# A planning constant for when the rows of a finished transfer may be used: 3.5 in place of 1.5 microseconds

## The chip, the cores and the metric

The kernel runs on one core of a Trainium2 chip. The metric is the device time of one execution in microseconds. Times are medians of several executions of the same program.

## The reference, cut to what matters

```python
def reference(x, w1d):                       # x: (1, 384, 384, 384) bf16, w1d: (1,)
    g = jnp.einsum("bhwc->bc", x) / (H * W)  # mean over all 147456 pixels, per channel
    s = _sigmoid(g * w1d[0])
    return x * s[:, None, None, :]           # every pixel scaled by its channel's gate
```

All of x (113 MB) has to be read before the first output can be written, and SBUF, the on-chip memory, holds only a part of it. So there are two passes: pass one reads everything and sums it, and keeps 367 of the 1152 rows per partition in SBUF (some of them packed four into three); pass two stores the kept rows, scaled, and loads, scales and stores the other 785 once more. A "row" below is 384 channels on 128 partitions, 98304 bytes.

## The kernel before

Loads and stores all go out on one queue, in the order in which the program adds them. The queue stops at the first transfer whose wait isn't met yet. A load into rows of the arena (the block of SBUF rows that all transfers share) waits until the store that last read them has landed; a store waits until VectorE has scaled its rows.

```python
def load(chunk, a, lo, hi):
    r0, n = chunk
    fl.add("SP",
        lambda: nc.sync.dma_start(out=arena[:, a : a + hi - lo, :], in_=view(xf, r0, n)[:, lo:hi, :]),
        writes=rows(a, hi - lo), dma=True)

def store(chunk, a, lo, hi):
    r0, n = chunk
    return fl.add("SP",
        lambda: nc.sync.dma_start(out=view(of, r0, n)[:, lo:hi, :], in_=arena[:, a : a + hi - lo, :]),
        reads=rows(a, hi - lo), dma=True)
```

`fl.add` works out the waits from the rows that a step reads and writes, so every order is safe. Which order it is, a plan decides while the program is built. It steps through pass two in its own time `now`, with a list `moves` of transfers that drain at a fixed rate:

```python
ROW, PER_LOAD, PER_STORE = 0.2267, 0.112, 0.061
LAT, SEEN, DT = 2.0, 1.5, 0.05
...
while True:
    ...                                   # VectorE: scale a landed chunk, or unpack a kept group
    while waiting and waiting[0][0] <= now:
        _, n, then, chunk, a, lo, known = waiting.popleft()
        known.append(store(chunk, a, lo, lo + n))
        moves.append([now + LAT, n * ROW + PER_STORE, then])
    ...
    while over and over[0][0] <= now:
        over.popleft()[1]()               # a store is over: its rows are idle, or a load has landed
    ...
    if got and todo < N_STREAM:
        n, a = max(got)                   # the longest run of idle rows
        n = min(n, CAP, N_STREAM - todo)
        ahead = backlog()
        if n >= BIG or n == N_STREAM - todo or (ahead < LOW and n >= 8) or ahead < LAST:
            load(STREAMED, a, todo, todo + n)
            ...
    if moves and moves[0][0] <= now:
        moves[0][1] -= DT
        if moves[0][1] <= 0:
            over.append((now + SEEN, moves.popleft()[2]))
    ...
    now += DT
```

`SEEN` is the time that the plan lets pass between the end of a transfer and the use of its rows. It holds for both kinds: for a store, until its rows may be loaded into, and for a load, until VectorE may be given its rows.

## Time and profile before

| | before |
|---|---|
| median, 6 executions | 722.3 us (721.88 to 723.66) |
| span of the profiled execution | 721.3 us |
| moved | 303.87 MB, 421 GB/s on average |
| first and last data packet of pass two | 271.8 and 718.9 us |

The prediction below shows the views and says how each is read. One thing in advance: a transfer is divided among 16 DMA engines. The trace has every packet (one partition's part of a transfer) with its start and its duration, and every increment of a transfer's semaphore; a transfer has landed when the last of the 16 increments stands. From these records I take three quantities: how long the packets of each size usually take, which packets took over 40 ns longer (called slow), and the time between the first and the last of the 16 increments of one transfer (called the spread).

### The profile page before, as it was taken

The numbers are of one execution on the slowest core, as the hardware profiler recorded it, in microseconds if no ns is written. First come the engines' busy times: TensorE is split into PE (matmuls) and PEld (weight loads), VectorE is DVE, ScalarE is ACT, GpSimd is POOL, SyncE is SP. The second block draws the span as 40 slices with busy tenths as digits, with TensorE's granted clock in tenths as the row PEclk, the third lists the DMA queues.
The fourth block names the chain that finished last, engine by engine and source line by source line (L and its number), as shares of the span: only waits on it lengthen the run. The fifth ranks groups of instructions, "written<-read, shape, count | busy, mean of one in ns | idle before, by whom it ended". The sixth has DMA issues, their size and how long they took to land.

```text
span 721.3 us, 3240 instructions
## 1 busy us (share of the span) xinstructions
PE 214.6 (30%) x1202; PEld 119.2 (17%) x1202; DVE 496.3 (69%) x470; ACT 115.4 (16%) x92; POOL 0.2 (0%) x4
## 2 busy tenths in 40 slices
PE   4677788897987770000000000000000000000000
PEld 2344445554543430000000000000000000000000
DVE  4600004788899819989799999999996992558500
ACT  3600003566677610002000000000000000000000
POOL 0000000000000000000000000000000000000000
PEclk9799999999899995555555555555555555555555
DMA  9999999999999978999999999999999999999997
GB/s 382 429 443 424 425 435 430 431 433 433 424 427 427 428 320 341 425 430 426 403 430 436 428 438 430 429 439 433 432 432 439 423 445 431 432 430 433 435 436 306
DMA packets 18882, 303.87 MB, mean 421 GB/s; under 512 B 2098, under 2 KB 2098, under 8 KB 4658
## 3 DMA queue, kind: packets, MB, share of 16 engines
q1 hardware_dynamic: 18864, 303.67, 98.6%
q8 instruction: 9, 0.15, 0.1%
q14 instruction: 7, 0.06, 0.0%
q10 hardware_dynamic: 2, 0.00, 0.0%
HBM read 190.41 MB, written 113.25 MB: 421 GB/s over the span
## 4 chain that ended last, share of the span: by engine, by line
DMA 55%; DVE 28%; PE 6%; ACT 5%; SPq 0%; issue 0%; another core or an unknown queue 0%; DVEq 0%
DMA arena<-in_x_dram 38%; DVE arena L441 19%; DMA out_dram<-arena 17%; DVE arena L265 6%; PE bank L241 6%; ACT arena L302 5%; DVE arena L271 3%; SPq L235 0%; ACT s_bf L432 0%; SPq L762 0%; DVEq L112 0%; SPq L106 0%
## 5 line engine op out<-in xcount | busy, mean ns | idle before, releaser
L441 DVE TENSOR_TENSOR arena<-arena,s_bf 128x1536 bf16<-128x1536 bf16 (+8 forms) x103 | 242.3, 2391 | 59.0 <-DMA arena<-in_x_dram 42.0
L265 DVE TENSOR_SCALAR arena<-arena 128x1536 uint16<-128x1536 uint16 (+2 forms) x247 | 145.5, 634 | 113.4 <-DMA arena<-in_x_dram 100.8
L241 PE MATMUL bank<-arena,ones 128*128 128x384 bf16 x1152 | 206.5, 341 | 52.7 <-DMA arena<-in_x_dram 52.6
L241 PEld LDWEIGHTS bank<-arena,ones 128*128 128x128 bf16 x1152 | 114.3, 102 | 144.6 <-DMA arena<-in_x_dram 58.7
L271 DVE TENSOR_TENSOR arena<-arena 128x1536 uint16<-128x1536 uint16 (+2 forms) x114 | 121.2, 1063 | 6.7 <-PE bank L241 4.4
L302 ACT ACTIVATE arena<-arena 128x3072 uint16<-128x3072 uint16 (+1 forms) x38 | 102.5, 2698 | 142.3 <-DVE arena L265 142.3
L514 PE MATMUL bank<-odd,ones 128*128 128x1 bf16 x1 | 0.2, 184 | 329.4 <-DVE odd L509 329.4
L514 PEld LDWEIGHTS bank<-odd,ones 128*128 128x128 bf16 x1 | 0.1, 103 | 329.8 <-DVE odd L509 329.8
L375 ACT COPY arena<-bank 128x512 uint32<-128x512 uint32 (+1 forms) x7 | 4.0, 571 | 61.8 <-DMA out_dram<-arena 61.6
L256 PE MATMUL bank<-ones,zeros 128*128 128x384 bf16 x48 | 8.3, 326 | 0.0
L302 ACT ACTIVATION_READ_ACCUMULATOR arena<-arena 128x1 f32 x38 | 7.1, 188 | 0.0
L256 PEld LDWEIGHTS bank<-ones,zeros 128*128 128x128 bf16 x48 | 4.7, 98 | 3.1
L375 ACT COPY bank<-arena 128x512 uint32<-128x512 uint32 (+1 forms) x7 | 3.6, 565 | 0.0
L432 ACT ACTIVATE s_bf<-bank,w_sc 128x384 bf16<-128x384 f32 x1 | 0.6, 581 | 15.4 <-PE bank L241 15.4
L735 ACT ACT_TABLE_LOAD x1 | 1.3, 1283 | 0.7 <-PEq L751 0.7
L332 DVE TENSOR_SCALAR w_sc<-bank 128x1 f32<-128x1 f32 x1 | 0.2, 159 | 1.1 <-PE bank L327 1.1
L322 DVE MEMSET ones<- 128x128 bf16 x1 | 0.2, 165 | 1.0 <-SPq L106 1.0
L327 PE MATMUL bank<-w_bf,ones 1*128 1x1 bf16 x1 | 0.2, 182 | 2.1 <-DMA w_bf<-in_w1d_dram 2.1
L327 PEld LDWEIGHTS bank<-w_bf,ones 1*128 1x128 bf16 x1 | 0.1, 100 | 2.1 <-DMA w_bf<-in_w1d_dram 2.1
L518 DVE CAST odd_i<-bank 128x1 int32<-128x1 f32 x1 | 0.2, 159 | 0.3 <-PE bank L514 0.3
L504 DVE TENSOR_REDUCE worst<-seen 128x1 f32<-128x38 f32 x1 | 0.2, 185 | 0.0
L509 DVE TENSOR_SCALAR odd<-worst 128x1 bf16<-128x1 f32 x1 | 0.2, 156 | 0.0
(5 smaller groups left out, 0.5 us busy)
## 6 DMA issues: line engine op xcount, KB each, us to landing
arena<-in_x_dram SPq DMA_DIRECT2D x15, 4608.0 KB, 33.9
arena<-in_x_dram SPq DMA_DIRECT2D x22, 1248.0 KB, 11.6
out_dram<-arena SPq DMA_DIRECT2D x8, 3072.0 KB, 30.3
arena<-in_x_dram SPq DMA_DIRECT2D x6, 3072.0 KB, 27.3
out_dram<-arena SPq DMA_DIRECT2D x12, 1248.0 KB, 11.8
out_dram<-arena SPq DMA_DIRECT2D x3, 4608.0 KB, 39.8
arena<-in_x_dram SPq DMA_DIRECT2D x3, 4512.0 KB, 37.9
out_dram<-arena SPq DMA_DIRECT2D x3, 4512.0 KB, 27.7
```

What stands on the lines that cost most here:

```text
L241: return nc.tensor.matmul(acc, lhsT=ones[:], rhs=arena[:, i, :], start=first, stop=last)
L256: lambda: nc.tensor.matmul(acc, lhsT=zeros[:], rhs=ones[:, None, :].to_broadcast([P, C // P, P]), start=False, stop=False),
L265: lambda: nc.vector.tensor_scalar(out=dst, in0=src, scalar1=s0, scalar2=s1, op0=op0, op1=op1),
L271: "DVE", lambda: nc.vector.tensor_tensor(out=dst, in0=a, in1=b, op=op), reads=reads, writes=writes
L302: lambda: nc.scalar.activation(out=y, in_=y, func=ACTF.Copy, accum_out=seen[:, 2 * k + i : 2 * k + i + 1]),
L322: fl.add("DVE", lambda: nc.vector.memset(ones[:], 1.0), writes=["ones"])
L327: lambda: nc.tensor.matmul(votes, lhsT=ones[0:1, :], rhs=w_bf[0:1, 0:1], start=True, stop=True),
L375: "ACT", lambda: nc.scalar.copy(dst.bitcast(u32), src.bitcast(u32)), reads=reads, writes=writes
L432: lambda: nc.scalar.activation(out=s_bf[:], in_=acc, func=ACTF.Sigmoid, scale=w_sc[:, 0:1]),
L441: lambda: nc.vector.tensor_tensor(out=v, in0=v, in1=s_bf[:, None, :].to_broadcast([P, n, C]), op=Op.mult),
L514: lambda: nc.tensor.matmul(votes, lhsT=ones[:], rhs=odd[:], start=True, stop=True),
L735: nc.scalar.preload_act_table(ACTF.Sigmoid)
```

## The change

The plan is to let 3.5 us pass before a store's rows count as free, so that loads come later in the queue, behind more stores, and hold it up less. The same constant also puts off the moment at which the plan counts a load as landed, and with it the order of VectorE's work.

```diff
-    LAT, SEEN, DT = 2.0, 1.5, 0.05
+    LAT, SEEN, DT = 2.0, 3.5, 0.05
```

## The prediction

> **What bounds the kernel now.** I read the page first (sections 2 and 4), then the busy time by stretch, then the waits of the DMA queue, then single microseconds where the transfer rate dips. The page's slices of one fortieth of the span:
>
> ```profile
> DVE  4600004788899819989799999999996992558500
> DMA  9999999999999978999999999999999999999997
> GB/s 382 429 443 424 425 435 430 431 433 433 424 427 427 428 320 341 425 430 426 403 430 436 428 438 430 429 439 433 432 432 439 423 445 431 432 430 433 435 436 306
> ```
>
> The DMA engines are full everywhere but in the first slice, at the turn from pass one to pass two (slices 15 and 16) and in the last one. VectorE is nearly full in the first two thirds of pass two, so it has to be kept in view. The same by stretch (busy time of each engine, then granted clock, DMA share, GB/s):
>
> ```profile
> 18.00:264.00 246.00, 200.62 (x1130) 111.83 (x1131) 130.13 (x180) 103.86 (x79) 0.00 (x0) 0.94 1.00 430
> 264.00:272.00 8.00, 5.25 (x32) 2.75 (x29) 2.02 (x3) 0.58 (x1) 0.00 (x0) 1.00 0.30 120
> 272.00:290.00 18.00, 0.00 (x0) 0.00 (x0) 17.96 (x13) 0.00 (x0) 0.00 (x0) 0.50 0.96 373
> 290.00:600.00 310.00, 0.18 (x1) 0.10 (x1) 292.79 (x249) 4.00 (x7) 0.00 (x0) 0.50 1.01 430
> 600.00:708.00 108.00, 0.00 (x0) 0.00 (x0) 45.12 (x14) 0.00 (x0) 0.00 (x0) 0.50 1.00 434
> 708.00:721.30 13.30, 0.00 (x0) 0.00 (x0) 0.00 (x0) 0.00 (x0) 0.00 (x0) 0.50 0.61 261
> ```
>
> Pass two (from 272 us) runs at 430 to 434 GB/s except in its first 18 us (373) and its last 13. TensorE's halved clock means nothing here: it has no work. VectorE is busy 293 of 310 us up to 600, but only 45 of 108 after that; it is done 40 us before the end.
>
> The waits of the queue that issues all transfers, in pass two (who waited for whom: us in total, times, longest):
>
> ```profile
> SPq L451 <- DVE arena L441: 240.5, 44, 29.0
> SPq L235 <- DMA out_dram<-arena: 145.2, 28, 17.3
> ```
>
> The second line is what the change aims at: 28 loads stand 145 us in the one in-order queue until the store of their rows has landed. That looks like a third of pass two, but the engines stay full meanwhile, since transfers issued earlier are still queued: these waits are hidden. Single microseconds at the dips (same columns):
>
> ```profile
> 277.00:278.00 1.00, 0.00 (x0) 0.00 (x0) 1.00 (x1) 0.00 (x0) 0.00 (x0) 0.50 1.12 313
> 278.00:279.00 1.00, 0.00 (x0) 0.00 (x0) 1.00 (x1) 0.00 (x0) 0.00 (x0) 0.50 0.78 215
> 279.00:280.00 1.00, 0.00 (x0) 0.00 (x0) 1.00 (x2) 0.00 (x0) 0.00 (x0) 0.50 0.82 240
> 280.00:281.00 1.00, 0.00 (x0) 0.00 (x0) 1.00 (x1) 0.00 (x0) 0.00 (x0) 0.50 0.86 227
> ...
> 347.00:348.00 1.00, 0.00 (x0) 0.00 (x0) 1.00 (x3) 0.00 (x0) 0.00 (x0) 0.50 0.96 255
> 716.00:717.00 1.00, 0.00 (x0) 0.00 (x0) 0.00 (x0) 0.00 (x0) 0.00 (x0) 0.50 0.34 147
> ```
>
> There the share is high and the rate low: the packets themselves are slow. At 277 to 281 us they are the 6144-byte packets of the first load of pass two (234 ns is usual, many took 446, some over 1000), at 344.5 to 350 the 9984-byte packets of another small load (375 usual, up to 1428). In the last microseconds the 16 engines end one after the other.
>
> **What the Trainium skill says.** "DMA: Bandwidth & Descriptors", section "Where 436 GB/s comes from", gives a ceiling of 435 GB/s for the 16 ports and says that for HBM to SBUF a limit of some 358 binds. The trace agrees with the first and not with the second: a 36864-byte packet takes 1364 ns on one of 16 engines, 432 GB/s, and whole stretches run at 434. Section "Anatomy of one DMA" puts a fixed cost of about 2 us on a transfer, most of it the receipt from the target memory. The trace shows less at the end of a store: the last data packet of the kernel ends at 718.87 us and the last increment of its semaphore stands at 719.20, 0.33 us later; the queue's next load starts 0.02 us after such an increment. Section "Queues, rings and completion order" says that each engine consumes its ring in order and that the increments of one transfer come from up to 16 engines separately. The trace agrees, and this matters: the 16 increments of one store come within 0.16 us at the start of pass two, but 2.5 us apart after the slow load at 277 us and 3.9 us apart after the one at 345 us, and they stay so to the end (715.34 to 719.20). The plan's constant must therefore cover 0.35 us of receipt plus this spread, which makes 3.5 us a more honest figure than 1.5.
>
> **The change part by part.** The constant is used only in the plan that is made while the program is built; nothing waits for it on the chip. It can act in one way, through the order and the sizes of transfers and VectorE instructions. Comparing the two built programs: TensorE, ScalarE and GpSimd have the same order, so have pass one and the start of pass two; the first difference is that the first load moves behind one more 8-row store. Everything up to about 275 us is out of reach.
> Bytes: in both plans 1152 rows (of 98304 bytes) are stored and 785 loaded in pass two, 190.4 MB. Nothing is saved there.
> Number of transfers in pass two: 82 before, 86 after (loads 30 to 32, stores 52 to 54). Packets of 6144 and 36864 bytes take 234 and 1364 ns, so a byte costs 0.0368 ns on one engine and a packet 8 ns besides; a transfer is 8 packets and a 9 ns increment per engine, some 0.075 us beyond its bytes. Four more make +0.3 us, on the path, since the engines are the bound.
> VectorE: the same instructions but for the cuts, in another order; no sum changes by more than about a microsecond of the 358 busy in pass two, and it has 93 us of slack.
> Distance of the loads: counting the rows that stand in the queue between a load and the nearest store that it waits for, before has 16 and 23 as its smallest, then 34, with a median of 49.5; after has 24, 26, 30, 34 and a median of 61. At 434 GB/s a row takes 0.2267 us, so the smallest cover goes from 3.6 to 5.4 us. Against the 0.35 us of receipt, both are enough on average; against a spread of 2.5 to 3.9 us among the engines 3.6 is short and 5.4 is not.
> What there is to win: the first packet of pass two starts at 271.81, the last ends at 718.87, 447.1 us. Every packet at the usual duration of its size sums to 443.7 us per engine. So 2.4 us went to slow packets and 1.0 to idle engines: 3.4 us, 0.47% of the time, is an estimate of the most that any order of the same transfers can win. The two loads with the least cover (16 and 23 rows) are just the two whose packets were slow, which suggests (two cases, no more) that more cover avoids some of it. I take a third of 3.4 us as won, -1.1, and +0.3 for the transfers, +0.3 for the first load's place: it now follows a store that VectorE gives out at 276.7 us, when the queue is nearly dry. Sum: -0.5 us, 723.0.
>
> **The rivals.** (1) A hole on account of VectorE: stores now stand ahead of loads and block them until VectorE has made them. I laid both orders out on the assumption that the engines never idle, with the traced VectorE durations (a scaling of 4, 12 and 16 rows 0.96, 2.55 and 3.35 us, a field operation 0.55). Past the first eight stores, where VectorE makes hardly more rows than the DMA takes in either order, the smallest slack of a store is near 3 us in both and grows to 10 to 30 us later; VectorE comes to its end some 12 us later than before, still over 25 us ahead of the last landing. For a 2% loss the queue would have to run dry for 14.5 us; I see no place for it. If I am wrong by a hole of some us, 726 to 728. (2) The slow packets come from where a load's rows lie in memory or from chance, not from its cover: then they stay, the gain is nil and the time 724; the plan has more small loads early, so they may even add 1 or 2 us. (3) The slow packets go altogether and the engines end together: 720.5. (4) The 145 us of waiting were a real cost: then some per cent would be gained; the full DMA row in the same stretches speaks against it.
>
> **Range and chances.** Executions of before lie within 722.4 and 723.7, so chance alone is +-0.6 us; with the gain of (3) and the losses of (1) and (2), 8 in 10 between 720.4 and 725.8. Faster by over 2% would need 14.5 us where 3.4 can be had: 0.5%. Slower by over 2%: 1%. Within 2%: 98.5%.
>
> **What would show it right or wrong.** Right: the same bytes, 4 more transfers, pass two from 290 us at 430 to 434 GB/s, the wait of loads for stores shorter in total while the time stays. The dip at 277 to 281 us gone or smaller, and the last microseconds steeper, would show that cover matters; a dip at the first load as before, that it doesn't. Wrong: a slice of pass two with a DMA row under 9 while VectorE is full (rival 1), a last VectorE instruction past 700 us, or a time outside 715 to 731.

## The result

The changed kernel took 723.75 us (median of 6, 723.43 to 723.99) against 722.3 of before. The ratio is 1.0015, 95% interval 1.0002 to 1.0028. The ratios are not quite the ratios of the medians. Run a second time, in a later job, the ratio was 1.0007 (0.9993 to 1.0021). So the change costs about one thousandth (+1.1 and +0.5 us in the two comparisons; the interval of the second holds 1), at the edge of what can be seen.

The slices of the changed kernel's page, the same three rows as of before:

```profile
DVE  4600004878999709999989899999899697033920
DMA  9999999999999978999999999999999999999997
GB/s 381 439 432 424 429 436 432 428 433 433 423 428 426 427 315 344 425 430 416 406 426 437 427 433 439 431 426 441 428 439 434 432 432 436 427 439 434 429 437 309
```

The DMA row is the same digit by digit. VectorE works later: its last slices have 0, 3, 3, 9 and 2 where before had 5, 5, 8, 5 and 0. The stretches of the changed kernel (us, then busy time of PE, weight loads, VectorE, ScalarE, GpSimd, then clock, DMA share, GB/s):

```profile
264.00:272.00 8.00, 5.16 (x31) 2.70 (x29) 2.11 (x3) 0.58 (x1) 0.00 (x0) 1.00 0.30 120
272.00:290.00 18.00, 0.00 (x0) 0.00 (x0) 17.97 (x13) 0.00 (x0) 0.00 (x0) 0.54 0.95 372
290.00:600.00 310.00, 0.19 (x1) 0.10 (x1) 294.04 (x250) 4.00 (x7) 0.00 (x0) 0.50 1.01 429
600.00:708.00 108.00, 0.00 (x0) 0.00 (x0) 43.90 (x14) 0.00 (x0) 0.00 (x0) 0.50 1.01 434
708.00:721.70 13.70, 0.00 (x0) 0.00 (x0) 0.00 (x0) 0.00 (x0) 0.00 (x0) 0.50 0.63 271
```

Rates of 372, 429 and 434 GB/s stand where 373, 430 and 434 stood. No hole has opened, and none has closed. The waits of the issuing queue in pass two:

```profile
SPq L451 <- DVE arena L441: 243.4, 49, 24.5
SPq L235 <- DMA out_dram<-arena: 135.3, 25, 21.2
```

The change did what it was meant to do: loads stood waiting for stores 135.3 us in place of 145.2. Ten microseconds of waiting less, and the time didn't fall: the DMA row is full in the same stretches, so during these waits the engines were working off earlier transfers. The dip at the first load of pass two:

```profile
277.00:278.00 1.00, 0.00 (x0) 0.00 (x0) 1.00 (x1) 0.00 (x0) 0.00 (x0) 0.50 1.04 436
278.00:279.00 1.00, 0.00 (x0) 0.00 (x0) 1.00 (x1) 0.00 (x0) 0.00 (x0) 0.50 1.08 436
279.00:280.00 1.00, 0.00 (x0) 0.00 (x0) 1.00 (x2) 0.00 (x0) 0.00 (x0) 0.50 1.00 246
280.00:281.00 1.00, 0.00 (x0) 0.00 (x0) 1.00 (x1) 0.00 (x0) 0.00 (x0) 0.50 0.72 227
281.00:282.00 1.00, 0.00 (x0) 0.00 (x0) 1.00 (x2) 0.00 (x0) 0.00 (x0) 0.50 0.86 190
```

The dip didn't go. It only starts 2 us later, where the load now stands.

The packets tell one thing that the prediction misread. Each of the 16 engines ends its part of a transfer with a 4-byte increment, so a packet that starts before the first such increment of a store cannot belong to a later transfer. By this count the dip begins on the 8-row store that stands just ahead of the load: its packets, of the same 6144 bytes, turn slow 1.5 to 1.7 us after the load was issued (up to 495 ns in place of 234), in all 14 profiles, and they make at least 0.52 of the 1.20 us per engine in before, 0.57 of 1.19 in after and 0.41 to 0.64 in every profile. The many packets of 446 ns are that store's; those of over 1000 ns are the load's.

### The profile page after: what moved, and what is told of

Same layout as the page of the kernel before. It is cut to its first block, busy times and chain, and to the rows that moved or that the text cites. A ratio compares the mean times of both kernels' runs of the same rounds, so it can differ in the third digit from the quotient of the medians.

```text
span 721.7 us, 3243 instructions
## 1 busy us (share of the span) xinstructions
PE 214.8 (30%) x1202; PEld 119.1 (17%) x1202; DVE 496.4 (69%) x470; ACT 115.4 (16%) x92; POOL 0.2 (0%) x4
## 4 chain that ended last, share of the span: by engine, by line
DMA 62%; DVE 22%; ACT 5%; PE 5%; issue 0%; SPq 0%; another core or an unknown queue 0%; DVEq 0%
DMA arena<-in_x_dram 45%; DMA out_dram<-arena 17%; DVE arena L441 14%; DVE arena L265 6%; ACT arena L302 5%; PE bank L241 5%; DVE arena L271 3%; SPq L235 0%; ACT s_bf L432 0%; SPq L451 0%; DVEq L112 0%; SPq L762 0%; SPq L106 0%
## 5 line engine op out<-in xcount | busy, mean ns | idle before, releaser
L441 DVE TENSOR_TENSOR arena<-arena,s_bf 128x1536 bf16<-128x1536 bf16 (+7 forms) x103 | 242.6, 2390 | 72.3 <-DMA arena<-in_x_dram 55.2
## 6 DMA issues: line engine op xcount, KB each, us to landing
out_dram<-arena SPq DMA_DIRECT2D x13, 1248.0 KB, 12.6
```

Source lines behind the costliest of these rows:

```text
L441: lambda: nc.vector.tensor_tensor(out=v, in0=v, in1=s_bf[:, None, :].to_broadcast([P, n, C]), op=Op.mult),
```

## The experiments

Every experiment leaves a profile, so the slow packets can be compared over all of them. The table gives, for the profiled executions of pass two, the time from first to last packet; what the packets would take at the usual duration of their sizes; and what slow packets took above it, all per engine, in us. The "first spell" is that at the first load of pass two (the 8-row store just ahead of it included), the "second spell" the one between 330 and 352 us.

| profiled execution | its time | pass two | usual sum | first spell | second spell |
|---|---|---|---|---|---|
| before | 723.04 | 447.1 | 443.7 | 1.20 | 1.04 |
| before again | 721.66 | 445.7 | 443.7 | 1.16 | 0.08 |
| first load moved | 721.71 | 445.7 | 443.7 | 1.32 | 0.22 |
| rows reversed | 721.97 | 446.1 | 443.7 | 1.25 | 0.25 |
| stores split | 726.10 | 450.2 | 447.0 | 1.31 | 0.90 |
| ninth load later | 722.10 | 446.1 | 443.7 | 1.34 | 0.02 |
| late part | 721.77 | 445.8 | 443.8 | 1.23 | 0.03 |
| late part again | 721.74 | 445.6 | 443.8 | 1.21 | 0.05 |
| after | 723.43 | 447.5 | 444.0 | 1.19 | 1.37 |
| after again | 722.71 | 446.9 | 444.0 | 1.38 | 1.31 |
| rest moved | 722.99 | 447.0 | 444.0 | 1.36 | 1.36 |
| early part | 723.88 | 448.0 | 444.1 | 1.34 | 1.43 |
| two loads later | 723.12 | 447.0 | 444.0 | 1.46 | 1.06 (330 to 360) |
| turn delayed | 744.92 | 447.5 | 444.0 | 1.21 | 1.20 (352 to 374) |

### First load moved: one part of the change alone

```diff
-            over.append((now + SEEN, moves.popleft()[2]))     # SEEN = 1.5
+            over.append((now + (3.5 if now < 12 else 1.5), moves.popleft()[2]))
```

The build differs from before in one place: the first load stands behind one more 8-row store.

> The kernel before with one part of the change: only the first load of pass two moves behind one more 8-row store; the other 81 transfers and all VectorE instructions stand as before. Theory A (the loss of about 1.1 us comes from the four extra transfers and the slow packets of the later plan): no difference from before, 1.000 within 0.05%. Theory B (the loss comes from the first load's new place, where the queue is nearly dry): ratio 1.001 to 1.002 (+0.7 to +1.5 us). In the profile the first load's packets are slow wherever it stands (both).

Measured: 722.42 us, ratio 1.0005 (0.9991 to 1.0019), five executions from 721.71 to 723.42. The first spell is there and as large as ever. The same microseconds of this kernel:

```profile
279.00:280.00 1.00, 0.00 (x0) 0.00 (x0) 1.00 (x2) 0.00 (x0) 0.00 (x0) 0.50 1.17 326
280.00:281.00 1.00, 0.00 (x0) 0.00 (x0) 1.00 (x1) 0.00 (x0) 0.00 (x0) 0.50 0.76 172
281.00:282.00 1.00, 0.00 (x0) 0.00 (x0) 1.00 (x1) 0.00 (x0) 0.00 (x0) 0.50 0.82 221
```

With 24 rows between the load and the store that it waits for in place of 16, the spell is just as large (1.32 us per engine against 1.20; without what is certainly the store's, 0.86 against 0.68). So the prediction's idea that more cover avoids it falls for this load. The time doesn't differ clearly from before, which fits theory A, but the interval also holds most of B's range.

### Rest moved: the change without that part

```diff
+            over.append((now + (1.5 if now < 12 else 3.5), moves.popleft()[2]))
```

> The change without the move of the first load: 86 transfers, the plan of after from there on. Theory A: as slow as after, ratio to before 1.001 to 1.002. Theory B: as fast as before, 1.000 within 0.05%. The landing spread of one transfer at the end is 2 to 4 us under both.

Measured: 723.44 us, ratio 1.0018 (1.0004 to 1.0032), the same as the whole change. That points to the rest of the plan, though the intervals of the two runs overlap. (This build also keeps the second load where before had it, so one small move of the change is in neither run.)

### Rows reversed: other addresses

```diff
-                load(STREAMED, a, todo, todo + n)
+                load(STREAMED, a, N_STREAM - todo - n, N_STREAM - todo)
```

The stores of these rows follow suit. Order and sizes stay.

> The plan of before, but pass two reads (and writes) the streamed rows from the other end: same order, same sizes, other addresses. Theory C (slow packets belong to certain addresses: rows 0 to 8 and about 102 to 115 of the streamed block were slow in both profiles): no slow packets near 345 us, they turn up at another load or not at all, and the spread of landings at the end falls from 3.9 us to 2.5 or less; time down by 0 to 3 us. Theory D (they belong to the moment or the place in the queue): slow packets again at the load near 277 and the one near 345 us, time unchanged within 0.1%.

Measured: 722.39 us, ratio 1.0008 (0.9994 to 1.0021), the five executions from 721.97 to 723.87. The first spell is there with wholly different rows (1.25), so it doesn't belong to the addresses that were read. (The rows of the arena that the loads fill are the same as before; they were not tested.) The second was small (0.25), as theory C has it, but it was as small in two other profiles with the old addresses (0.22 and 0.08, below), so that says nothing. The time didn't move. Theory C falls for the first spell and stays untested for the second.

### Stores split: what does a transfer cost?

```diff
+        if hi - lo >= 16:
+            mid = (lo + hi) // 2
+            written.append(store(chunk, a, lo, mid))
+            a, lo = a + mid - lo, mid
         return fl.add("SP", ...)
```

> The plan of before with every store of 16 rows or more cut in halves until each piece is under 16 rows: 127 transfers in pass two in place of 82, same bytes and same place. If a transfer costs 0.075 us beyond its bytes and the engines are the bound, +45 x 0.075 = +3.4 us (ratio 1.0047). If the cost of one more transfer is hidden, nothing; if it costs more than the packets show (a receipt, the queue's 0.35 us of issuing), +5 us or more.

Measured: 726.1 us, ratio 1.0044 (1.0031 to 1.0058): +3.2 us (2.2 to 4.2) for 45 transfers, 0.071 us each (0.05 to 0.09), as expected. The stretch that has only large transfers in before shows it as a lower rate (the same stretch of before stood at 434):

```profile
290.00:600.00 310.00, 0.19 (x1) 0.10 (x1) 293.18 (x249) 4.00 (x7) 0.00 (x0) 0.50 1.01 428
600.00:708.00 108.00, 0.00 (x0) 0.00 (x0) 45.12 (x14) 0.00 (x0) 0.00 (x0) 0.50 1.01 430
```

The sum of the usual packet durations rises by 3.3 us, from 443.7 to 447.0. So the packets alone account for the cost, and the four extra transfers of the change are worth +0.28 us: four times 0.071.

### Early part and late part: where in the rest?

```diff
# early part
+            over.append((now + (3.5 if now < 100 else 1.5), moves.popleft()[2]))
# late part
+            over.append((now + (1.5 if now < 60 else 3.5), moves.popleft()[2]))
```

The first build is the plan of after up to about 390 us of the span; the second is the plan of before up to the ninth load (342 us), which it puts behind one more store, and goes on with the longer constant.

> The plan of after up to about 390 us (3.5 us in the plan's first 100 us), 1.5 us from there on: 88 transfers in pass two. Theory A1 (four transfers more cost 0.3 us, and the rest of the loss comes from the slow spell of loads near 340 us, which is longer or more frequent in the plan of after): as slow as after or 0.1 us more, ratio 1.0015 to 1.002, with a spell of over 0.8 us per engine between 330 and 350. Rival A2 (the loss is made in the later part of pass two, by the other cuts and the last stores): ratio 1.0005 or less (six transfers are 0.45 us).

> The plan of before up to 340 us, then 3.5 us: 84 transfers. A1: ratio 1.000 to 1.0005 (two transfers are 0.15 us). A2: 1.0012 to 1.002.

Measured: early part 723.85 us, ratio 1.0010 (0.9996 to 1.0024), all five executions between 723.31 and 723.88; late part 721.77 us, ratio 0.9985 (0.9972 to 0.9999), all five between 721.61 and 722.42. The two ratios are of the same job and the same before. The executions of the two builds don't overlap, so what is lost is lost in the early part, as A1 has it, and the late part of the change didn't lose anything; it even came out ahead, which neither theory had. The early part's ratio is under the expected one, and its interval holds 1, so its loss against before is not shown by its time alone.

### Before and after again

No edit; both kernels once more, in the same job as the last two.

> The kernel before, unchanged, against itself: how far the same program strays. Ratio 1.000 within 0.1%. A1: the spell near 345 us is there in some executions and not in others; where this profile's spell is small (under 0.3 us per engine), its time is near 721.8, where it is near 1 us, 723.

> The kernel after, unchanged, on the same chip as the others: ratio 1.001 to 1.002 again. A1: a spell of 0.8 us per engine or more between 330 and 350 us for the third time with this plan. If the spell is missing here and the time is still above 723, A1 falls.

Measured: before against itself 0.9996 (0.9983 to 1.0010), executions from 721.66 to 723.76; after 723.33 us, 1.0007 (0.9993 to 1.0021), executions from 722.71 to 723.65. After's ratio is below the 1.001 to 1.002 that was expected, and its interval holds 1: there is little to tell apart. The stretch from 340 to 350 us, first the profile of before that the prediction read, then of before again, of after, of after again, and of the late part:

```profile
340.00:350.00 10.00, 0.00 (x0) 0.00 (x0) 9.93 (x12) 0.00 (x0) 0.00 (x0) 0.50 1.01 385
```

```profile
340.00:350.00 10.00, 0.00 (x0) 0.00 (x0) 9.93 (x12) 0.00 (x0) 0.00 (x0) 0.50 1.00 424
```

```profile
340.00:350.00 10.00, 0.00 (x0) 0.00 (x0) 9.93 (x11) 0.00 (x0) 0.00 (x0) 0.50 0.99 370
```

```profile
340.00:350.00 10.00, 0.00 (x0) 0.00 (x0) 9.93 (x12) 0.00 (x0) 0.00 (x0) 0.50 1.01 385
```

```profile
340.00:350.00 10.00, 0.00 (x0) 0.00 (x0) 9.93 (x12) 0.00 (x0) 0.00 (x0) 0.50 1.01 428
```

The same program, before, once loses 1.04 us per engine in this stretch at 385 GB/s and once 0.08 at 424, and the two executions took 723.04 and 721.66 us. The DMA share is 1.0 in all: a slow packet counts as busy, and only the rate beside it shows the loss. With the early plan of after, the spell was there in four profiles of four (1.31 to 1.43); after again, too, had it, but took 722.71 us in its profiled execution, so the last sentence of that expectation did not come into play.

### Turn delayed: does the second spell belong to a moment?

```diff
+    for _ in range(36):
         fl.add("ACT", lambda: nc.scalar.activation(out=s_bf[:], in_=acc, func=ACTF.Sigmoid, ...), ...)
```

> The plan of after, with the sigmoid between the passes computed 36 times instead of once (the same values, about 20 us more between the passes): all of pass two runs 20 us later. Theory E (loads are slow at a certain time, about 335 to 350 us, whatever they load): the spell stays at 335 to 350 and hits the loads that are then on their way, the 4-row and 13-row loads that used to run at 317 to 327. Theory F (it is the place in the queue, the tenth and eleventh load, that makes them slow): the spell moves with them to 355 to 370 us, still over 1 us per engine. Time 743 to 745 us under both.

Measured: 744.92 us (one look, no state). The spell moved with the plan. In this kernel, 340 to 350 us runs undisturbed, and 361.5 to 371.5 us has it (1.20 us per engine between 352 and 374):

```profile
340.00:350.00 10.00, 0.00 (x0) 0.00 (x0) 9.71 (x9) 0.00 (x0) 0.00 (x0) 0.50 1.02 434
...
361.50:371.50 10.00, 0.00 (x0) 0.00 (x0) 9.93 (x11) 0.00 (x0) 0.00 (x0) 0.50 1.00 388
```

Theory E, a fixed moment, falls.

### Two loads later: does it belong to two certain loads?

The tenth and eleventh load of after's plan go out two stores later (the lines that keep the two counts and send what is held are left out):

```diff
+                if n_loads in (10, 11):
+                    held.append((n_stores + 2, (STREAMED, a, todo, todo + n)))   # load() after two more stores
+                else:
                     load(STREAMED, a, todo, todo + n)
```

> The plan of after with one thing changed: the tenth and eleventh load of pass two (20 and 8 rows) stand behind two more 13-row stores, so that they are read from about 350 us on in place of 339 to 349. Theory E: the spell is gone or under 0.4 us per engine, and the time falls by 1.0 to 1.5 us against after, to 0.999 to 1.0003 of before. Theory F or any that lays the spell to these loads themselves: spell still over 1 us, ratio 1.001 to 1.002.

Measured: 723.04 us, ratio 1.0001 (0.9986 to 1.0016), executions from 722.93 to 723.76. The time fits E, the profile doesn't: the spell came later and is still 1.06 us, and it now falls mostly on the 13-row load that follows the two, which ran at full rate in after. The two loads were read from about 346 us on, not from 350 as expected. The stretch from 350 to 356 us, of this kernel and then of after:

```profile
350.00:356.00 6.00, 0.00 (x0) 0.00 (x0) 3.47 (x2) 0.00 (x0) 0.00 (x0) 0.50 1.00 369
```

```profile
350.00:356.00 6.00, 0.00 (x0) 0.00 (x0) 6.00 (x5) 0.00 (x0) 0.00 (x0) 0.50 1.03 436
```

So it isn't these two loads in themselves (F) either. (F had the size of the spell right and the time wrong; E the reverse.) The ratio of 1.0001 comes with a before that strayed widely in this job (721.18 to 724.55), so I don't read a gain from it.

### Late part again, and its one swap alone

> The kernel of the late part again, since it came out faster than before (0.9985): if that was no chance, ratio 0.998 to 0.9995 once more, no spell of slow loads between 330 and 352 us (under 0.2 us per engine) and a median near 721.8; if chance, a ratio of 1.000 and a spell in some executions.

> The plan of before with one swap: its ninth load (13 rows, the one that was slow near 345 us in some executions) stands behind one more store of 11 rows, as in the late part; 82 transfers, the same VectorE order. If that swap alone is what made the kernel of the late part faster: no spell (under 0.2 us per engine between 330 and 352), median 721.5 to 722.0, executions within 0.8 us of each other, ratio 0.9980 to 0.9995. If the later cuts made it faster, or chance: ratio 0.9995 to 1.0005, executions between 721.7 and 723.7 as those of before.

The second of these is the plan of before with the ninth load held back by one store (the edit above with the ninth in place of the tenth and eleventh, and one store in place of two).

Measured: late part again 721.99 us, ratio 0.9989 (0.9973 to 1.0005), no second spell (0.05), executions from 721.74 to 722.33 and one of 723.32. The swap alone: 722.55 us, ratio 0.9995 (0.9982 to 1.0009), no spell in its profile (0.02), but executions from 721.69 to 723.45. The late part stands at 0.9985 and 0.9989; one interval excludes 1 and the other just doesn't. It is ahead of both kernels by what I'd call a probable thousandth. The swap takes the ninth load's cover from 23 to 34 rows, so it is also the one test of the prediction's idea on that load; three profiles with the swap have no second spell (0.02, 0.03, 0.05), but of the five without it two have hardly one (0.08 and 0.22). The swap alone is not shown to be the cause: its executions stray as those of before do, though its one profile has no spell. Either the spell comes back in some executions, or something else varies too.

## Why the prediction was right, and where it wasn't

- What bounds the kernel, and that 2% were out of reach: right. The 145 us of waiting loads were hidden; when they shrank to 135 us, the time didn't follow. Nothing breaks the ceiling of 3.4 us on any gain: it was worked out from an execution of 723.04 us, and the fastest of all executions took 721.18. In the second profile of the same program the same sum is 2.0 us (445.7 less 443.7).
- The time of 723.0 and the range: 723.75 lies within, but the sign was wrong. A gain of 0.5 us was worked out, and the change lost 0.5 to 1.1. That 723.0 came so near is in part luck: the sum started from 723.5, the median of the three executions of before that were known. The six have 722.3, and over the later jobs before took 721.18 to 724.63, so the chance of +-0.6 us was also too narrow. From 722.3 the same sum gives 721.8, 1.9 us under what was measured.
- The step that failed is the term of -1.1 us, "a third of 3.4 us as won" from slow packets by more cover. That the two least covered loads were the two slow ones did not hold as a rule: the first spell is as large with 24 rows of cover as with 16 (1.32 and 1.20 us) and begins on the store ahead of the load, which the prediction took for the load's own packets; and in after the second spell falls on loads with 55 and 95 rows between and is larger (1.37). For the ninth load of before alone the idea stays open. Nor is the term fixed: in before the second spell was 1.04 in the profile that I read and 0.08 in another. The other sign that the prediction named, a steeper end, says nothing either: the last store's spread was 3.86 us in before and 3.28 in after, but 2.70 and 2.73 in their second profiles.
- The term of +0.3 us for four transfers: right. The split stores give 0.071 us for each, +0.28 for four.
- The term of +0.3 us for the first load's place: not seen (ratio 1.0005, interval across 1). It may be there.
- Rival 2, that the spells don't depend on cover and more small early loads add to them, at 724, came nearest. The mean second spell over the five profiles with the plan of before in that stretch (before, before again, first load moved, rows reversed, stores split) is 0.50 us, over the four with that of after 1.37. The difference of 0.87 and the 0.28 for transfers make 1.15 us, which is about the +1.1 of the first comparison, if twice the +0.5 of the second. That is a sum over single profiled executions, so it is an account that fits, not a proof.
- Rival 1, a hole on account of VectorE: didn't occur. VectorE's last store was issued at 690.5 us in place of 677.9, 12.6 us later, where "some 12" were expected, and the rates stayed (429 and 434 GB/s).
- Small slips: the median cover after is 62.5 rows, not 61, and the first slice, called not full, has a 9 in the DMA row (its rate is 382 GB/s). Nothing rests on them.
- What stays open: what makes a load's packets slow for some 5 to 15 us. It isn't the addresses read nor the cover (first spell), nor a fixed moment nor two certain loads (second spell). The rows of the arena and the neighbours in the queue were not tested. Nor did any run separate the constant's two uses: the plan built with 3.5 us for stores alone has 90 transfers in pass two, with 3.5 us for loads alone 85, and neither was timed.

## What to carry to other kernels

Here 10 us less waiting in the issuing queue brought nothing, because the engines never ran dry; look at the rate of the transfers in the same stretch before counting such waits as a cost. Where the transfer engines are full, a new order of the same bytes can win only what idle engines and slow packets lost, so sum that first: it was 0.47% here, which ruled out a gain of some per cent before anything was run. Ask of a slow stretch which transfer its packets belong to: here part of it was a store's. And read a second profile of the same program before explaining a feature of one microsecond, since the one that looked like a pattern here was absent in the next execution.

## What the Trainium skill lacked or had wrong

- "DMA: Bandwidth & Descriptors", section "Where 436 GB/s comes from", says without a condition that for HBM to SBUF some 358 GB/s binds. One core alone moved loads and stores at 434 GB/s for over 100 us (600 to 708 us of before), near the page's other figure of 435. Elsewhere the page has it right: it keeps 358 for two cores streaming at once.
- The same page breaks a fixed cost of about 2 us down for transfers issued from GpSimd ("Anatomy of one DMA — SWDGE (gpsimd) path"). It has no such account for transfers issued from SyncE, as here, nor the cost of one more in a full queue: the last increment stood 0.33 us after the last data packet, and a transfer more cost 0.071 us (45 more: ratio 1.0044), the packets' own time.
- No page tells how far the 16 engines drift apart, and that the spread stays while the queue is full: spread of one store's increments 0.16 us at the start of pass two, 3.86 us at its end in before, 3.28 us in after.
- None tells of spells in which packets take up to several times their usual duration: 1.2 to 1.5 us per engine at the first load of pass two in all 14 profiles, of which at least 0.41 to 0.64 us lie on the store just ahead of it, and a second one of 0.0 to 1.4 us that the same program has in one execution and not in another (1.04 and 0.08).
